# A sorted-attention and token-mixing kernel: a new order of its units, k' turned by 128-column weights, the last output row in halves

## Chip, cores and metric

The kernel runs on one core of a Trainium2 chip. Its time is the device time of one execution in microseconds (us); lower is better. Each engine (TensorE or PE, VectorE or DVE, ScalarE or ACT, GpSimd or POOL, SyncE or SP) runs its own list of instructions in order and waits on semaphores for the others. TensorE writes to PSUM, which has eight banks; VectorE and ScalarE copy results from there to SBUF.

## What is computed

For 4 batches and 8 heads, keys and values of 8 blocks of 96 positions are mixed by an 8 x 8 matrix that five rounds of row and column normalization have made; each block of queries then attends to its mixed block. The result is the input of a token mixer.

```python
for _ in range(5):                      # P = sort_net, 4 x 8 x 8 x 8
    P = exp(P - P.max(-1))
    P = P / P.sum(-1);  P = P / P.sum(-2)
k_sorted = einsum('bhij,bhjcd->bhicd', P, k_b)      # q, k, v: 4 x 8 x 768 x 64
v_sorted = einsum('bhij,bhjcd->bhicd', P, v_b)
attn = softmax(q_b @ k_sorted^T / 8)                # in blocks of 96
x = attn @ v_sorted                                 # 4 x 768 x 512
W_tok = (x @ w_q) @ (x @ w_k)^T / 8                 # 768 x 768 for each batch
out = relu(W_tok @ x) @ w_out                       # 4 x 768 x 512, float32
```

## The kernel before

The program is a list of units, `ORDER` (lines 20 to 54), which the loop at lines 661 to 671 walks once. A unit is `kind batch number : engine : bank`; a capital letter other than R, D, I is work of TensorE, with the PSUM bank that it writes (K, Y, V, S, P and H take two banks from there on). A small letter is mostly the copy that takes the result of the same capital out of that bank; A is ScalarE, D VectorE, G GpSimd, S SyncE. So `K20:6` turns the keys of batch 2, heads 0 and 1, into banks 6 and 7, and `k20:A:6` lets ScalarE copy them out. Each engine gets its units in the order of the list, and waits are put in by the framework for every tile, bank and buffer that two units share. The order thus decides everything: which unit of TensorE stands behind which, which engine copies, which bank is used again how soon, and what is queued behind what on a DMA queue.

The kinds, in the order in which a batch goes through them:

- `l`: a load by GpSimd's queue of half the heads of q, k or v of a batch (`lk2a`: k, batch 2, first half); I: the loads of q of batch 0 by SP. `lp` and `lo` load the mixer's weights.
- A, a, c, B, u, n: the normalization and the matrices M that sort (VectorE and ScalarE alternate: a is exp, c the sums and quotients). Z are idle products with zeros, beside that chain.
- p, z (copies), Q, q: queries, two heads at a time, turned by TensorE.
- K, k: sorted and turned keys. V, v: sorted values, which R (six transfers by SP) puts into VT; for batch 0 Y, y, F, f do the same on TensorE.
- S, e: scores of five head pairs and blocks at a time, and exp to E (line 363).
- P, r, x: E times the values, the reciprocal of the row sums and the quotient to X (lines 387, 392). There are five such groups, the fifth of 8 instead of 14 products.
- T, t (batches 0 and 1) or D (batches 2 and 3, a transposing transfer by SP, line 398): X turned to XT. D20 needs the groups 0 to 2, D21 the groups 2 to 4.
- J, j: the mixer's q' and k' (qkT, 64 rows each) for half of the positions, from all four parts of XT. d copies k' to other partitions (qD).
- W, w (`u_W`, line 423): k' turned back, block by block, by a product of a 96-column piece of qkT, taken as weights, with part of an identity.
- G, g, H, h: k'^T x, and its product with q', then the relu, to mixT.
- O, o, s: the output rows, six of 128 positions for a batch: four products of 512 columns, a copy to a buffer `ot` (four of them, used in turn, each for two rows), and a store. Batches 0 to 2 store two rows at a time (512 KB), batch 3 each row by itself (256 KB). `osplit` (line 464) reads a number over 9 as a half row: `O325` is batch 3, row 5, second half.

Batches overlap: the attention of batch b+1 stands between the mixer units of batch b. A check on the row sums (`guard`, line 495) and a path for its failure, which doesn't run here, close the program.

## Time and profile before

| | |
|---|---|
| time before, median of 3 runs | 98.08 us (97.96 to 98.28) |
| the profiled execution | 98.33 us |
| its span, first to last instruction | 96.4 us |
| TensorE busy | 86.3 us, 1333 products |
| weight loads (PEld, beside TensorE) | 58.7 us |
| VectorE, ScalarE, GpSimd busy | 72.6, 68.8, 43.1 us |
| mean granted clock of TensorE | 0.991 |
| read from and written to HBM | 20.19 and 6.29 MB |

In the profile's rows, `ps<-wo,mixT 128*128 128x512` is a product that writes PSUM from weights of 128 partitions by 128 columns and 512 columns of data; behind `|` stand the busy time in us and the mean length of one in ns, then the idle time before them with what ended it. Products overlap, so that the distance of their starts, not their length, is what one costs. `SPq` is SP's queue, `POOLq` GpSimd's. A tile's name stands without its buffer number. Line 154 is the helper of all products, lines 158, 160 and 162 are the copies of ScalarE, GpSimd and VectorE.

### The profile page before, as it was taken

The page shows a single profiled execution, that of the slowest core. Times are in us where ns is not written, and L with a number is a line of the kernel's source. Part 1 is how long each engine was busy: PE and PEld are TensorE (multiplying, and loading weights), DVE is VectorE, ACT ScalarE, POOL GpSimd, SP SyncE. Part 2 cuts the span into 40 slices and gives each one's busy share as a digit, 9 for nine tenths or more (in the row PEclk, how much of TensorE's full clock was granted, in tenths as well). Part 3 has the DMA queues.
Part 4 walks back from the last instruction along what each step waited for, and adds up shares of the span by engine and source line. Part 5 has one row for each costly group of instructions (what it writes and reads, how often), then busy time and mean ns, then how long its engine had stood idle before and what let it go on. Part 6 is the DMA issues. An engine that isn't in the chain of part 4 may idle for free.

```text
span 96.4 us, 3206 instructions
## 1 busy us (share of the span) xinstructions
PE 86.3 (90%) x1333; PEld 58.7 (61%) x1342; DVE 72.6 (75%) x141; ACT 68.8 (71%) x96; POOL 43.1 (45%) x70
## 2 busy tenths in 40 slices
PE   4999587999899999999999999899969999999930
PEld 2344177788787687845778687674756545644400
DVE  2767896988999469999877999987796773645520
ACT  5177629998979999796989888999746090466220
POOL 6996309700999993049998006000004021950000
PEclk9999999999999999999999999999999999999996
DMA  0899999999999999999999999379953899785992
GB/s 10 266 353 227 203 203 203 203 203 207 195 275 216 209 203 207 202 204 249 250 225 204 202 204 289 124 208 206 205 206 70 199 118 413 289 352 221 396 366 112
DMA packets 24655, 21.44 MB, mean 222 GB/s; under 512 B 7296, under 2 KB 22720, under 8 KB 24640
## 3 DMA queue, kind: packets, MB, share of 16 engines
q0 software_dynamic: 12720, 10.36, 65.5%
q1 hardware_dynamic: 11200, 9.05, 35.5%
q10 hardware_dynamic: 720, 1.84, 4.8%
q8 instruction: 10, 0.16, 0.7%
q14 instruction: 5, 0.04, 0.1%
HBM read 20.19 MB, written 6.29 MB: 275 GB/s over the span
## 4 chain that ended last, share of the span: by engine, by line
PE 55%; DVE 16%; ACT 12%; DMA 10%; issue 3%; SPq 0%; DVEq 0%; ACTq 0%
PE ps L154 55%; DMA XT<-X 5%; DMA XT<-in_q_dram 5%; DVE X L392 4%; ACT E L363 4%; ACT KT L158 3%; DVE QT L162 2%; ACT Vs L158 2%; DVE VT L162 1%; DVE Vs L162 1%; DVE M L253 1%; DVE XT L162 1%; ACT mixT L460 1%; ACT Qn L158 1%; DVE tmp L193 1%
## 5 line engine op out<-in xcount | busy, mean ns | idle before, releaser
L363 ACT ACTIVATE E<-ps 96x960 bf16<-96x960 f32 (+1 forms) x28 | 24.3, 905 | 2.2 <-PE ps L154 1.6
L154 PE MATMUL ps<-wo,mixT 128*128 128x512 bf16 x88 | 22.8, 380 | 0.4
L392 DVE TENSOR_TENSOR X<-ps,Rall 96x896 bf16<-96x896 f32 (+1 forms) x20 | 20.1, 1006 | 0.7
L160 POOL COPY Qn<-Qn 128x768 bf16<-128x768 bf16 x10 | 8.1, 831 | 16.9 <-DMA Qn<-in_q_dram 16.9
L162 DVE COPY ot<-ps 128x512 f32<-128x512 f32 (+1 forms) x16 | 10.8, 687 | 4.8 <-PE ps L154 4.5
L154 PEld LDWEIGHTS <-mixT 128*128 128x128 bf16 x96 | 8.3, 98 | 9.1 <-issue 0.8
L154 PE MATMUL ps<-VT,E 96*128 96x65 bf16 x256 | 11.2, 193 | 0.3
L154 PEld LDWEIGHTS <-KT 64*128 64x128 bf16 (+1 forms) x288 | 8.4, 97 | 4.5 <-issue 2.2
L154 PEld LDWEIGHTS <-E 96*128 96x128 bf16 x256 | 9.7, 97 | 2.1 <-issue 0.4
L158 ACT CAST KT<-ps 128x768 bf16<-128x768 f32 x13 | 10.2, 808 | 0.9 <-DVE Rall L387 0.4
L154 PE MATMUL ps<-QT,KT 64*128 64x96 bf16 x256 | 9.3, 204 | 1.1 <-ACT KT L158 0.8
L160 POOL COPY qD<-qkT 64x384 bf16<-64x384 bf16 x6 | 3.0, 505 | 15.0 <-ACT qkT L158 12.8
L460 ACT ACTIVATE mixT<-ps 128x1024 bf16<-128x1024 f32 x7 | 7.1, 1027 | 3.5 <-PE ps L154 3.5
L253 POOL TENSOR_TENSOR M<-PTR,m_p 128x512 bf16<-128x512 bf16 x6 | 7.9, 1318 | 3.6 <-ACT PTR L158 3.5
L158 ACT COPY ot<-ps 128x512 f32<-128x512 f32 x9 | 5.3, 587 | 5.1 <-PE ps L154 4.7
L154 PE MATMUL ps<-idb,Qn 128*128 128x128 bf16 x96 | 7.7, 220 | 1.1 <-DVE Pm L190 1.0
L154 PE MATMUL ps<-fil 128*128 128x512 bf16 x25 | 8.2, 482 | 0.1
L154 PE MATMUL ps<-M,Kn 128*64 128x128 bf16 x192 | 7.8, 221 | 0.1
L162 DVE CAST KT<-ps 128x768 bf16<-128x768 f32 x7 | 6.7, 955 | 1.2 <-PE ps L154 1.1
L154 PEld LDWEIGHTS <-Qn 128*128 128x128 bf16 x96 | 5.7, 98 | 3.0 <-ACT Qn L158 2.1
L158 ACT CAST Vs<-ps 128x1024 bf16<-128x1024 f32 x7 | 7.0, 1012 | 0.6 <-PE ps L154 0.5
L387 DVE RECIPROCAL Rall<-ps 96x14 f32<-96x14 f32 (+1 forms) x20 | 4.6, 228 | 3.5 <-PE ps L154 2.2
(84 smaller groups left out, 142.9 us busy)
## 6 DMA issues: line engine op xcount, KB each, us to landing
Vn<-in_v_dram POOLq DMA_DIRECT2D x8, 384.0 KB, 9.6
Kn<-in_k_dram POOLq DMA_DIRECT2D x8, 384.0 KB, 11.4
out_dram<-ot SPq DMA_DIRECT2D x5, 512.0 KB, 4.7
VT<-Vs SPq DMA_DIRECT2D x18, 132.0 KB, 5.0
Qn<-in_q_dram POOLq DMA_DIRECT2D x6, 384.0 KB, 11.4
XT<-in_q_dram SPq DMA_DIRECT2D x2, 768.0 KB, 5.7
out_dram<-ot POOLq DMA_DIRECT2D x2, 512.0 KB, 7.4
out_dram<-ot ACTq DMA_DIRECT2D x2, 512.0 KB, 2.8
```

Of the source, the lines that this page charges most:

```text
L154: nc.tensor.matmul(o, w, x, is_transpose=t, start=start, stop=stop, skip_group_check=True)
L158: nc.scalar.copy(o, i)
L160: nc.gpsimd.tensor_copy(o, i)
L162: nc.vector.tensor_copy(o, i)
L193: nc.vector.reduce_sum(tmp, (Pm if n == 1 else Pv).rearrange("p i j -> p j i"), axis=AX.X)
L253: ENG[e].tensor_tensor(out=M[b % 2][:, h0:h0 + hn], in0=src.unsqueeze(2).to_broadcast([P, hn, SP, NB]), in1=m_p.unsqueeze(1).unsqueeze(3). ...
L363: nc.scalar.activation(E[b % 2][:, n, 0:2 * w * BLK].rearrange("p (t a c) -> p a t c", a=2, c=BLK), PS[0:BLK, bank:bank + 2, 0:w * BLK].re ...
L387: nc.vector.reciprocal(Rall[:, b, n, :, 0:w], avps(bank, w)[:, :, :, D])
L392: nc.vector.tensor_mul(xo.rearrange("p (a t d) -> p a t d", a=2, d=D), avps(bank, w)[:, :, :, 0:D], Rall[:, b, n, :, 0:w].unsqueeze(3).to_ ...
L460: nc.scalar.activation(o, i, ACT.Relu)
```

## The change

There are three edits. `ORDER` is replaced as a whole: the same units, but for the three named below, in another order, with other banks and in 66 places another engine. In it, heads 4 to 7 of batch 0 go first and not last; some y, k and v copies of batches 0 and 1 change between ScalarE and VectorE; s01 and s10 go from GpSimd's queue to SP's, other stores and copies between SP, ScalarE and VectorE; the loads come in another sequence (lq3b is the last one, not lk3b). There are 25 idle products in place of 26 (Z53 for Z54). In `u_W`, three of four pieces of qkT are taken as weights of 128 columns and write 128 rows, of which 96 are used. The last row of batch 3, now row 5 in place of row 3, is computed, copied and stored in two halves of 256 columns (O325, O315 and their o and s).

```diff
--- before.py
+++ after.py
@@ -18,39 +18,39 @@
 VHEAD = set()
 
 ORDER = """
-i00:G i02:D I00:S A00:0 Z04:1 Z15:1 Z25:1 lv0b I01:S lk0a c00:D a01:A i03:G c01:D lv0a a02:A:0 lk0b
-c02:D z11:A lv1b lv1a a03:A Q01:0 Z33:1 c03:D lk1a lq1b lk1b z10:A a04:A c04:D z12:A Q00:2 Z43:1
-q01:D:0 a05:A z13:A c05:D q00:A:2 Z54:1 Q03:0 Z62:1 q03:D:0 B00:2 Q02:3 n01:D:2 n00:D:2 n03:D:2
-u00:A:2 K01:4 K00:0 q02:D:3 n11:G n10:G k01:A:4 Y03:6 k00:D:0 y03:A:6 S02:4 n02:D:2 e02:A:4 Y00:0
-K02:2 Y02:6 y00:A:0 k02:D:2 Y01:4 y02:A:6 S00:0 y01:D:4 lp K03:2 e00:A:0 S01:6 k03:D:2 F00:4 lq1a
-e01:A:6 F01:5 f00:D:4 S06:2 S05:0 e06:A:2 f01:D:5 P00:6 e05:A:0 S03:2 r00:D:6 x00:D:6 V12:4 e03:A:2
-P01:0 r01:D:0 x01:D:0 v12:A:4 S04:6 F03:2 F02:3 e04:A:6 R15:S V11:4 f02:D:3 V10:0 v11:A:4 f03:D:2
-P02:6 p12:G v10:A:0 r02:D:6 x02:D:6 R12:S p13:G P04:2 R14:S K11:4 n20:G T00:0 r04:D:2 x04:D:2
-k11:A:4 R13:S Q12:1 P03:6 R11:S t00:A:0 q12:D:1 lk2a K13:2 r03:D:6 x03:D:6 R10:S Q13:1 k13:A:2 lv2b
-K12:4 U00:0 k12:A:4 lv2a K10:2 z01:D:0 T03:6 q13:D:1 k10:A:2 T02:7 t03:D:6 U01:4 p11:G T01:5 t02:D:7
-z02:A:4 S16:2 S14:0 t01:D:5 lo e16:A:2 S15:6 Q11:4 e15:A:6 p10:G J01:5 q11:D:4 J00:2 e14:A:0 n21:G
-S13:6 j00:D:2 j01:A:5 Q10:0 e13:A:6 W01:1 lq2a W00:1 P14:2 P13:4 w00:A:1 d01:G r14:D:2 x14:D:2
-q10:A:0 K20:6 lq2b G00:1 r13:D:4 x13:D:4 k20:A:6 lq3a S11:2 G01:1 e11:A:2 d00:G K21:6 g00:D:1 S10:4
-lk2b k21:D:6 H01:0 e10:A:4 h01:D:0 V20:2 V21:4 v20:A:2 V22:6 v21:D:4 P10:0 v22:A:6 R21:S T13:2
-r10:D:0 x10:D:0 R20:S H02:4 S12:6 O02:3 R25:S e12:A:6 h02:D:4 R23:S H00:0 o02:A:3 P12:6 R22:S
-h00:A:0 O03:3 p21:G r12:D:6 x12:D:6 R24:S t13:A:2 P11:4 lk3a O04:0 r11:D:4 x11:D:4 p20:G O00:2
-o04:A:0 lv3a p23:A T10:0 o00:D:2 lv3b Q21:1 p22:A Q20:4 q21:D:1 T11:2 n31:G q20:A:4 T12:5 t11:D:2
-O05:1 t12:A:5 o03:D:3 lq3b t10:D:0 S22:6 S20:4 e22:A:6 S21:2 lk3b o05:D:1 J11:0 p30:G e21:A:2 Q23:1
-j11:D:0 J10:6 p31:G q23:D:1 e20:A:4 Q22:7 j10:D:6 W11:1 n30:G Q30:0 q22:A:7 K22:4 q30:D:0 K23:2
-k22:A:4 Q31:0 s01:G k23:D:2 W10:1 P21:6 d10:G w10:A:1 d11:D S23:4 q31:D:0 S24:2 e23:A:4 O01:1
-r21:D:6 x21:D:6 e24:A:2 S25:4 G10:0 o01:D:1 e25:A:4 K31:6 K30:2 k31:D:6 G11:0 k30:A:2 P22:4 g10:D:0
-S26:2 r22:D:4 x22:D:4 V30:0 e26:A:2 P23:6 v30:A:0 H10:2 r23:D:6 x23:D:6 V31:4 h10:A:2 R30:S p33:G
-S31:0 R31:S v31:D:4 e31:A:0 p32:G V32:6 H12:2 v32:A:6 S32:0 h12:D:2 R33:S Q33:4 Q32:5 e32:A:0 R32:S
-K32:6 q33:D:4 R34:S P24:2 k32:A:6 K33:0 r24:D:2 x24:D:2 R35:S k33:A:0 P20:6 q32:D:5 D21:S H11:2
-S35:0 r20:D:6 x20:D:6 h11:A:2 O14:5 e35:A:0 S33:2 o14:D:5 D20:S S36:6 O13:4 e33:A:2 P31:0 s00:S
-e36:A:6 S34:2 r31:D:0 x31:D:0 P34:6 e34:A:2 O10:5 r34:D:6 x34:D:6 P32:2 o10:A:5 S30:0 r32:D:2
-x32:D:2 P33:6 e30:A:0 J20:5 J21:0 r33:D:6 x33:D:6 j20:A:5 P30:2 d20:G j21:A:0 W20:5 r30:D:2 x30:D:2
-d21:G W21:5 D31:S O12:6 w20:A:5 G21:5 o13:D:4 D30:S G20:5 o12:D:6 O11:4 g20:D:5 s11:S H20:6 s02:S
-H22:2 h20:A:6 H21:0 h22:D:2 O15:5 o11:A:4 O21:6 o15:D:5 h21:A:0 s10:G O20:7 J30:0 J31:1 j30:D:0
-O25:5 d30:G j31:D:1 d31:S W30:4 o20:D:7 W31:4 O22:1 w30:A:4 w31:A:4 o25:D:5 o21:A:6 G31:0 s12:A
-G30:0 s20:A O23:6 o22:A:1 g30:A:0 H30:0 o23:D:6 H31:4 h30:A:0 H32:2 h31:D:4 O24:7 s21:S h32:A:2
-O31:6 o24:A:7 O32:2 o31:D:6 s22:S O34:3 s31:A o32:D:2 O35:6 s32:A o34:A:3 O30:7 o35:D:6 s34:S O33:3
-s35:A o30:D:7 s30:S o33:A:3 s33:S
+i00:G i02:D I01:S A00:0 lk0b I00:S Z04:1 lv0b c00:D a01:A lv0a c01:D Z15:2 i03:G a02:A:0 lk0a c02:D
+z13:A lv1a Z25:0 lv1b a03:A c03:D lk1b z12:A Q03:2 a04:A Z33:3 c04:D Q02:0 z10:A Z43:3 q03:D:2 a05:A
+z11:A Z53:1 c05:D Q00:2 Z62:1 q00:A:2 q02:D:0 B00:1 Q01:2 n02:D:1 n03:D:1 q01:A:2 K02:4 n01:D:1
+K03:6 k02:A:4 n00:D:1 Y02:2 u00:D:1 k03:A:6 Y01:4 y02:D:2 lq1b n11:G Y00:0 y01:A:4 S05:6 y00:D:0
+K01:2 e05:A:6 Y03:4 n10:G F02:0 y03:D:4 k01:A:2 K00:6 f02:D:0 S04:4 k00:A:6 F00:2 lp e04:A:4 S03:0
+f00:D:2 F01:6 e03:A:0 F03:7 lq1a f01:D:6 S01:4 S02:2 f03:D:7 lk1a e01:A:4 V10:0 P03:6 v10:D:0
+e02:A:2 K13:4 S00:2 r03:D:6 x03:D:6 k13:A:4 R11:S P01:0 e00:A:2 V11:4 r01:D:0 x01:D:0 K12:6 v11:A:4
+p12:G P02:2 k12:A:6 r02:D:2 x02:D:2 n21:G R13:S S06:4 P00:0 e06:A:4 R12:S V12:6 r00:D:0 x00:D:0
+P04:4 p13:G v12:A:6 U00:2 Q12:3 lk2a q12:A:3 R15:S T02:6 r04:D:4 x04:D:4 Q13:7 p11:G R14:S T00:0
+z01:A:2 q13:D:7 T01:1 lv2a t02:A:6 R10:S T03:2 t00:D:0 S15:4 t01:D:1 lv2b S16:6 U01:3 e16:A:6 K11:0
+z02:D:3 p10:G e15:A:4 K10:6 k11:D:0 Q11:3 lo t03:A:2 S14:4 q11:D:3 Q10:0 lq2a e14:A:4 J01:1 q10:D:0
+k10:D:6 S13:2 S12:4 e13:A:2 J00:0 j01:D:1 P14:6 e12:A:4 j00:D:0 S11:2 r14:D:6 x14:D:6 W01:1 d00:G
+W00:1 P12:4 w00:A:1 n20:G S10:6 e11:A:2 r12:D:4 x12:D:4 G01:1 G00:1 e10:A:6 lk2b K21:2 g00:D:1 P13:4
+n31:G d01:D k21:A:2 H00:6 r13:D:4 x13:D:4 H02:0 h00:A:6 V20:2 n30:G h02:D:0 v20:A:2 H01:6 T13:4 lq3a
+T12:5 h01:A:6 R21:S V21:2 t12:D:5 V22:0 R20:S v21:A:2 P11:6 O05:5 r11:D:6 x11:D:6 v22:A:0 R23:S
+O01:2 p21:G R22:S o05:D:5 P10:6 R25:S p20:G o01:A:2 O02:0 r10:D:6 x10:D:6 R24:S t13:A:4 lq2b Q20:1
+lv3b K22:4 q20:D:1 K20:6 k22:A:4 lv3a T11:2 k20:D:6 Q21:1 t11:A:2 O03:4 lk3a q21:D:1 o02:A:0 lk3b
+T10:5 S21:0 t10:D:5 S20:2 e21:A:0 S22:6 o03:D:4 J11:5 p30:G e20:A:2 K23:0 p31:G J10:4 k23:D:0
+j11:A:5 e22:A:6 Q30:2 d11:G Q31:5 q30:D:2 P20:0 p23:A p22:G q31:D:5 O04:6 r20:D:0 x20:D:0 j10:A:4
+lq3b Q23:7 W11:4 Q22:5 q23:A:7 o04:D:6 W10:4 P21:0 w10:A:4 q22:D:5 S26:2 S25:6 e26:A:2 r21:D:0
+x21:D:0 G11:4 e25:A:6 G10:4 S23:2 g10:D:4 P24:6 e23:A:2 d10:D S24:0 r24:D:6 x24:D:6 V30:4 e24:A:0
+V32:2 v30:D:4 V31:6 v32:A:2 K31:0 v31:D:6 R31:S P22:4 k31:A:0 K30:2 R30:S r22:D:4 x22:D:4 H10:0
+k30:A:2 R34:S O00:6 h10:A:0 R35:S S31:2 o00:D:6 S32:4 R32:S e31:A:2 P23:0 p33:G R33:S K32:6 r23:D:0
+x23:D:0 e32:A:4 D20:S O10:2 p32:G k32:A:6 Q33:3 o10:D:2 H12:0 s02:S q33:A:3 S30:4 H11:6 D21:S Q32:2
+e30:A:4 h11:D:6 O11:3 h12:A:0 q32:D:2 K33:4 o11:D:3 P31:6 k33:A:4 S33:0 r31:D:6 x31:D:6 s10:S
+e33:A:0 S34:2 s01:S P30:4 s00:S e34:A:2 r30:D:4 x30:D:4 O13:0 P32:6 S36:4 S35:2 r32:D:6 x32:D:6
+e36:A:4 J20:1 e35:A:2 J21:4 D30:S j20:A:1 P33:6 j21:D:4 d20:G P34:2 r33:D:6 x33:D:6 W20:1 W21:1
+O12:4 w20:A:1 o13:A:0 G20:5 r34:D:2 x34:D:2 o12:A:4 G21:5 d21:D O14:0 D31:S g20:A:5 H20:4 o14:D:0
+H22:2 h20:A:4 H21:6 s11:S O15:1 h21:D:6 O20:0 h22:D:2 O22:6 o15:D:1 O21:7 o22:A:6 s12:S J31:6 J30:1
+j31:A:6 W31:2 j30:D:1 O23:6 w31:A:2 d31:A d30:D W30:2 o23:D:6 G31:1 w30:A:2 G30:1 o20:D:0 s21:A
+O24:6 o21:A:7 g30:D:1 s20:S H30:0 o24:D:6 H31:2 h30:A:0 H32:4 h31:D:2 O25:7 h32:A:4 O31:6 o25:D:7
+O33:4 s22:A o31:A:6 O32:5 s31:A o33:A:4 O34:6 o32:D:5 s33:A O30:7 s32:S o34:D:6 O325:5 s34:S o30:A:7
+O315:4 o325:A:5 s30:S o315:A:4 s325:S s315:S
 """
 
 
@@ -422,7 +422,8 @@
 
     def u_W(b, n, bank):
         for i in range(4 * n, 4 * n + 4):
-            mm(PS[0:BLK, bank, i * DH:(i + 1) * DH], qkT[b % 2][:, i * BLK:(i + 1) * BLK], idb[:, DH:P])
+            w = BLK if i % 4 == 3 else P
+            mm(PS[0:w, bank, i * DH:(i + 1) * DH], qkT[b % 2][:, i * BLK:i * BLK + w], idb[:, DH:P])
 
     def u_w(b, n, e, bank):
         i0, i1 = (4 * n, 4 * n + 4) if b == B - 1 else (0, NB)
```

## Prediction

> **What bounds the kernel now.** I read the page's busy times first, then the busy time by stretches, then the chain that ended last, then the timelines of TensorE and of SP's queue around its long pieces.
>
> ```profile
> span 96.4 us, 3206 instructions
> ...
> PE 86.3 (90%) x1333; PEld 58.7 (61%) x1342; DVE 72.6 (75%) x141; ACT 68.8 (71%) x96; POOL 43.1 (45%) x70
> ```
>
> TensorE is busy for 86.3 of 96.4 us, so a new order can only take away its gaps, or add some. The stretches say where the gaps are; behind each pair of bounds stand the length and then the busy time of PE, PEld, DVE, ACT and POOL.
>
> ```profile
> 12.14:34.00 21.86, 20.24 (x459) 17.33 (x460) 18.59 (x32) 19.03 (x26) 14.07 (x17) 1.00 1.28 213
> 55.00:71.57 16.57, 15.30 (x302) 11.35 (x303) 14.71 (x24) 14.66 (x18) 1.59 (x2) 1.00 1.04 203
> 80.10:92.50 12.40, 12.29 (x83) 6.08 (x83) 7.01 (x10) 5.00 (x9) 3.74 (x8) 1.00 0.83 334
> ```
>
> From the first product after the normalization (12.14 us) to 34 us TensorE is idle for 1.62 us, from 55 to 71.57 for 1.27 us, and in the last 12.4 us for 0.11 us. The granted clock is 1.00 throughout (the column behind POOL). The second stretch has two pieces with a name:
>
> ```profile
> 60.54 0.61 PE L154 MATMUL ps<-Vn,M 128*128 128x128 bf16 x8 [0.35 <-DVE X L392]
> ...
> 63.96 0.59 PE L154 MATMUL ps<-VT,E 96*128 96x65 bf16 x14
> ...
> 66.47 1.04 PE L154 MATMUL ps<-wo,mixT 128*128 128x512 bf16 x4
> 67.34 0.60 PE L154 MATMUL ps<-VT,E 96*128 96x65 bf16 x14
> ...
> 70.30 0.59 PE L154 MATMUL ps<-VT,E 96*128 96x65 bf16 x14
> 71.57 1.47 PE L154 MATMUL ps<-XT,wqk 128*128 128x384 bf16 x8 [0.68 <-DMA XT<-X]
> ```
>
> The first row is V32, which waits 0.35 us for x23 to leave bank 6. Then come P20, the output row O13 (67.34 - 66.47 = 0.87 us for its four products), P31, P33, and last J20 with J21. The chain that ended last shows why J20 is late: it goes through the second transposing transfer of batch 2 (D20), which takes 5.19 us of it.
>
> ```profile
> 66.33 5.19 DMA XT<-X
> ```
>
> **Part 1, the order on TensorE: switches.** A row of the trace gives the price of going from one shape of product to another.
>
> ```profile
> 33.05 0.39 PE L154 MATMUL ps<-QT,KT 64*128 64x96 bf16 x10
> 33.37 0.51 PE L154 MATMUL ps<-idb,Qn 128*128 128x128 bf16 x6
> 33.72 0.51 PE L154 MATMUL ps<-idb,qkT 128*96 128x64 bf16 x8
> 34.06 0.84 PE L154 MATMUL ps<-VT,E 96*128 96x65 bf16 x22
> 34.84 0.36 PE L154 MATMUL ps<-M,Kn 128*64 128x128 bf16 x6
> ```
>
> ```profile
> 48.37 0.81 PE L154 MATMUL ps<-QT,KT 64*128 64x96 bf16 x30
> 49.11 0.50 PE L154 MATMUL ps<-XT,wqk 128*128 128x384 bf16 x2
> ```
>
> Ten score products that stand alone (S13) hold TensorE from 33.05 to 33.37, 0.32 us. Three such units in a row (S22, S20, S21) hold it for 0.74 us. If one unit costs a and leaving the scores costs s, a + s = 0.32 and 3a + s = 0.74, so a = 0.21 and s = 0.11; I take 0.095 for a switch, since a semaphore's share is in it. The kinds fall into three classes: S and H (weights on 64 rows), K, Y, G and the first U (weights of 64 columns), and all others. Counting changes of class along the list gives 69 in the old order and 74 in the new one. Five more at 0.095 are **+0.47 us**; in gaps they cost nothing, so the other end is 0.
>
> **Part 2, k' by 128-column weights (u_W).** 24 of the 32 weight loads grow from 96 to 128 columns.
>
> ```profile
> L154 PEld LDWEIGHTS <-E 96*128 96x128 bf16 x256 | 9.7, 97 | 2.1 <-issue 0.4 <-ACT E L363 0.2
> ```
>
> ```profile
> L154 PE MATMUL ps<-idb,qkT 128*96 128x64 bf16 x32 | 2.3, 208 | 0.0
> ...
> L154 PEld LDWEIGHTS <-qkT 128*96 128x96 bf16 x32 | 2.0, 124 | 0.3
> ```
>
> A load of 128 columns takes 97 ns here, one of 96 columns 124 ns. The spacing agrees: in the timeline above, 8 W products with one product's length of 0.21 us (208 ns) taken off 0.51 us come every 0.043 us, and 22 P products behind 128-column weights (0.84 us) every 0.030 us. So each longer load spares up to 0.013 us, 24 of them at most 0.31 us. Only a product whose load follows another W product shows it, so I take **-0.15 us**, with 0 and -0.31 as ends. The Trainium skill says the opposite in "TensorE: Matmul & The Clock Gate", section "LDWEIGHTS (loading the stationary operand)": a load's time is its columns divided by 1.2, so that 128 columns cost 107 ns against 80 ns. By that rule the edit would cost an estimated 24 x 0.027 = 0.64 us, and the total below would be 0.79 us higher; the two rows contradict it.
>
> **Part 3, the wait of J20.** P33's 14 products at 0.030 us end at 70.30 + 0.43 = 70.73 us, and J20 starts at 71.57: 0.84 us lost, until D20 has landed. In the old order the work from P20 (63.96) to J20 is 70.73 - 63.96 = 6.8 us long, while P20's way through x20 and D20 takes 71.57 - 63.96 = 7.6 us. In the new order the last such way begins at P23, and until J20 TensorE has three output rows, as before, five score units and three P, but also K32, K33, Q33 and Q32, and one more H, for one P less of eight products. The two K are 24 products at (0.36 - 0.21)/5 = 0.03, the two Q 12 at (0.51 - 0.21)/5 = 0.06: 1.4 us more work, and 0.4 us of switches that Part 1 counts. That makes 8.2 us or more against 7.6 us. I take **-0.8 us**; the other end is 0, if the transfers come later (second rival).
>
> **Part 4, the wait of V32.** V32 goes to bank 2, which e23 on ScalarE frees, and stands ahead of P22 and P23, so x23 no longer holds it up: **-0.35 us**, other end 0. Next in line is V31, now behind x24, the short one. I give nothing for the smaller gaps of that stretch.
>
> **Part 5, the opening.** The idle products drop from 26 to 25; they lie beside the normalization's chain on VectorE and ScalarE, which has the same steps in the same order with one QT copy at the same place in it, so 12.14 us stays. Without that cover each would be worth one 512-column product. Behind it work is moved between engines. Of the large copies VectorE takes over y00, y02, y03, k10, k11 and v10, and gives away y01, k00, k02 and k03.
>
> ```profile
> L162 DVE CAST KT<-ps 128x768 bf16<-128x768 f32 x7 | 6.7, 955 | 1.2 <-PE ps L154 1.1
> ...
> L162 DVE CAST Vs<-ps 128x1024 bf16<-128x1024 f32 x2 | 2.4, 1213 | 0.0
> ```
>
> One more KT copy and a Vs copy are +0.96 + 1.21 = +2.2 us; five small ones against four make it 2.2 to 2.7. VectorE then has 20.8 to 21.3 of the 21.86 us. ScalarE loses about as much and its chain of E comes sooner. I take **0**: the lower end is -0.6, a third of the gap of 1.62, the upper one is the first rival.
>
> **Part 6, the end.** Behind TensorE's last product only ScalarE's copy of the last row and SP's store are left. The row is now copied and stored in halves, both copies on ScalarE and both stores on SP.
>
> ```profile
> L158 ACT COPY ot<-ps 128x512 f32<-128x512 f32 x9 | 5.3, 587 | 5.1 <-PE ps L154 4.7 <-ACT ot L158 0.5
> ...
> L158 ACT CAST wk<-ps 96x256 bf16<-96x256 f32 x2 | 0.6, 370 | 3.2 <-PE ps L154 3.2
> ```
>
> The last copy shrinks from 587 to some 370 ns, -0.22 us. TensorE's eight half products are the same columns as four whole ones. A half store moves half as much, but SP has one store more to issue: between -0.2 and +0.15, I take 0. Together **-0.2 us**. Other transfers and copies moved to other engines between 71.57 and 92.5 us (d31 to ScalarE, stores between SP and ScalarE) lie beside a TensorE that is 99% busy from 80.10 us on; I cost them at nothing, and at their own length if that cover is gone.
>
> **The sum:** +0.47 - 0.15 - 0.8 - 0.35 + 0 - 0.2 = -1.03 us. The profiled execution took 98.33 us (96.4 us of span and 1.9 us around it), so its counterpart would be 97.3; it lies 0.25 us above the median of 98.08, which goes to 97.05, and I forecast **97.0 us**. Its own range is 96.3 to 97.7 us: one of the larger parts, 0.6 to 0.8 us, at its other end.
>
> **Rivals.** *VectorE becomes the bound in the opening (slower).* It now waits 21.86 - 18.59 = 3.27 us in that stretch. With 2.2 to 2.7 us more work only 0.6 to 1.1 us of waiting fit in. Against it: a longer queue waits less. If the waits stay, the stretch grows by 2.4 us: 99.4 us. It decides from about 0.9 us of waits on.
>
> *SP's queue makes J20 and J31 late (slower).* Old and new stores and transposes lie in this queue:
>
> ```profile
> 64.58 3.33 SPq L398 DMA_TRANSPOSE XT<-X  x2
> 67.96 0.74 SPq L485 DMA_DIRECT2D out_dram<-ot  x1
> 72.85 3.44 SPq L398 DMA_TRANSPOSE XT<-X  x2
> 76.39 2.15 SPq L485 DMA_DIRECT2D out_dram<-ot  x2
> ```
>
> ```profile
> XT<-X SPq DMA_TRANSPOSE x1, 4.0
> XT<-X SPq DMA_TRANSPOSE x1, 5.2
> out_dram<-ot SPq DMA_DIRECT2D x1, 512.0 KB, 4.7
> ```
>
> D21, issued at 64.58, lands at 68.6; D20, issued at 66.33, at 71.5; s00, issued at 67.96, at 72.7. So in line each transpose takes 2.9 us and a store 1.2 us. The new order has D20 s02 D21 s10 s01 s00 D30 D31 in one line; s01 and s10, until now POOL's, wait in front of D30 and D31. From an issue at about 62.5 us (it waits for x22 and for the last VT transfer, where D21 now waits for x24 until 64.58; an estimate) that is 4.0 + 3 x 2.9 + 4 x 1.2 = 17.5, so D31 lands at 80.0 us, about when J31 is due by my forecast (J30 starts at 80.10 now, and an output row of 0.87 us has moved ahead of it). The gain is gone when it lands after 81; at 0.5 us more for each of the four, 82.0 us, the time is 98.9 us.
>
> *Nothing changes:* the waits of Parts 3 and 4 come back elsewhere, on copies that now stand behind others: 97.05 + 0.8 + 0.35 = 98.2 us. For it speaks that DVE and ACT are busy for 89% and 88% of the stretch where both lie. *The opening gains too:* 96.2 us, or less. *Loads cost by their columns:* 128/96 of 124 ns is 165 ns, 41 ns more for each of 24, +1.0 us in place of -0.15: 98.2 us. This is the rule of the Trainium skill named in Part 2; the 97 ns row speaks against it.
>
> **How the numbers follow.** Forecast 0.52, a gain in the opening as well 0.08, loads by their columns 0.02, no change 0.12, VectorE 0.14, SP's queue 0.12. A change under 0.3% (0.3 us) can't be told from none here. Faster is 0.60, the same 0.14, slower 0.26. The range from 96.0 to 99.0 us leaves out about 0.15, above all the first rival.
>
> **What would show it.** Right: J20 and V32 without a wait, J31 at about 80 us, W's loads at 97 ns, 74 changes of class, and P14 at 34 us as before. Wrong: P14 much later than 34 us with VectorE full from 12 to 34 us (first rival), J20 or J31 released by the transfer of X (second), or new waits of TensorE for ScalarE and VectorE between 45 and 70 us (third).

## The result: slower by 6%

| | before | after |
|---|---|---|
| median, same chip | 98.28 us (97.96 to 99.04, 5 runs) | 104.24 us (103.80 to 106.41, 5 runs) |
| ratio, 95% interval | | 1.0605 (1.0551 to 1.0659) |
| profiled execution, its span | 98.33 us, 96.4 us | 103.8 us, 101.6 us |
| mean granted clock of TensorE | 0.991 | 0.975 |

The forecast was 97.0 us. The page of the changed kernel has the span, the busy times and the row of the granted clock:

```profile
span 101.6 us, 3221 instructions
...
PE 87.3 (86%) x1335; PEld 59.5 (59%) x1345; DVE 73.8 (73%) x142; ACT 69.9 (69%) x99; POOL 41.3 (41%) x66
...
PEclk9999999999999999999999999999995899999996
```

TensorE is busy for 1.0 us more, and the span is 5.2 us longer, so most of the loss is idle time. This execution is the fastest of the five runs of the changed kernel. One new thing stands in the clock's row: a 5, three quarters of the way through. The view by stretches says where the time is:

```profile
12.07:35.96 23.89, 20.83 (x463) 17.17 (x462) 20.40 (x34) 20.21 (x26) 13.94 (x18) 1.00 1.23 204
35.96:55.00 19.04, 17.58 (x315) 13.28 (x318) 15.11 (x23) 14.92 (x20) 13.52 (x17) 1.00 1.24 207
55.00:73.20 18.20, 17.65 (x344) 13.06 (x344) 16.47 (x28) 15.69 (x21) 2.15 (x3) 1.00 0.99 173
73.20:79.80 6.60, 4.66 (x45) 3.02 (x42) 3.55 (x6) 2.71 (x5) 0.95 (x2) 0.74 0.99 330
...
86.08:97.80 11.72, 11.66 (x84) 5.97 (x83) 6.26 (x10) 6.25 (x11) 0.00 (x0) 1.00 0.62 251
```

Behind the bounds and the length stand, as in the prediction, the busy times of PE, PEld, DVE, ACT and POOL, and then the granted clock. Up to P14 (35.96 us) TensorE is idle for 3.06 us; before it was 1.62 us up to the same unit. From there to 55 us it is idle for 1.46 us. Then comes the stretch that the change was to shorten, and it is good: 0.55 us in 18.2, where there were 1.27 us in 16.57. From J20 (73.20 us) on everything is lost at once: 1.94 us idle in 6.6 us, and the granted clock is 0.74 on average. The end is as full as before. The long waits of TensorE have one row each in its timeline:

```profile
22.35 0.53 PE L154 MATMUL ps<-M,Kn 128*64 128x128 bf16 x12 [0.98 <-DMA Kn<-in_k_dram]
...
35.96 0.42 PE L154 MATMUL ps<-VT,E 96*128 96x65 bf16 x8 [1.47 <-DMA VT<-Vs]
...
40.65 0.27 PE L154 MATMUL ps<-qD,Ab 64*128 64x256 bf16 x1 [0.67 <-DVE qD L162]
...
59.70 1.51 PE L154 MATMUL ps<-Vn,M 128*128 128x128 bf16 x24
...
73.20 0.50 PE L154 MATMUL ps<-XT,wqk 128*128 128x384 bf16 x2
75.42 1.57 PE L154 MATMUL ps<-XT,wqk 128*128 128x384 bf16 x6 [1.72 <-DMA XT<-X]
76.78 1.42 PE L154 MATMUL ps<-VT,E 96*128 96x65 bf16 x22
```

These are K13, P14, H02, the three V units of batch 3 (no wait between them now: V32's is gone), and J20 with J21. J20's first two products start at 73.20 without a wait, and the third, which reads the part of XT that D21 fills, stands until 75.42 us. Behind it 22 P products take 1.23 us (from 76.78 to 78.01, where W starts); at the 0.030 us for each of the old profile they would take 0.66 us.

The chain that ended last now runs through those transfers. The second number is the length of a piece:

```profile
7.19 15.11 DMA Kn<-in_k_dram
...
22.35 0.55 PE ps L154 x12
...
22.91 0.80 ACT KT L158
...
26.88 1.02 ACT Vs L158
...
29.32 6.59 DMA VT<-Vs
...
35.96 1.56 PE ps L154 x40
...
39.39 1.22 DVE qD L162
...
69.11 6.26 DMA XT<-X
```

The load of k for heads 4 to 7 of batch 1 releases K13; ScalarE's copies behind it end with the last Vs copy at 27.9 us; the last of the six VT transfers (R10) is issued at 29.32 us and lands 6.6 us later, at 35.91; P14 starts. Before, it was issued at 27.51 us and landed at 32.67, 1.4 us ahead of P14, which started at 34.06. Then d01, a copy of VectorE, takes 1.2 us, and at the end D21 takes 6.3 us. (By the code a d copies q', rows 0 to 63 of qkT, for the H products, and not k', as the list of kinds has it.) SP's queue shows what stood ahead of D21 (start, length of the issue):

```profile
66.81 1.58 SPq L398 DMA_TRANSPOSE XT<-X  x1
68.44 0.57 SPq L486 DMA_DIRECT2D out_dram<-ot  x1
69.11 2.29 SPq L398 DMA_TRANSPOSE XT<-X  x1
71.59 2.47 SPq L486 DMA_DIRECT2D out_dram<-ot  x3
74.33 7.14 SPq L398 DMA_TRANSPOSE XT<-X  x2
```

D20, the store s02, D21, three more stores, D30 and D31: the line that the second rival named. The granted clock around J21 stands third from the end, in stretches of 1 us:

```profile
75.00:76.00 1.00, 0.58 (x4) 0.38 (x4) 0.00 (x0) 0.00 (x1) 0.00 (x0) 0.99 1.10 455
76.00:77.00 1.00, 1.00 (x8) 0.52 (x7) 0.00 (x0) 0.47 (x1) 0.40 (x1) 0.50 0.97 397
...
78.00:79.00 1.00, 0.78 (x13) 0.72 (x12) 0.97 (x2) 0.28 (x1) 0.00 (x0) 0.50 1.06 343
79.00:80.00 1.00, 1.00 (x5) 0.30 (x6) 0.96 (x3) 0.89 (x3) 0.65 (x1) 0.80 1.26 283
```

For 3.4 us TensorE runs at half its clock, so the wait for D21 is paid nearly twice: once as idle time, and then up to 1.7 us as slow products. Two stretches of the kernel before are needed for the sum:

```profile
71.57:80.10 8.53, 8.48 (x78) 4.74 (x80) 5.91 (x9) 3.97 (x6) 1.55 (x3) 1.00 0.82 163
34.00:55.00 21.00, 20.50 (x369) 15.14 (x369) 18.38 (x30) 18.61 (x25) 13.40 (x18) 1.00 1.28 217
```

Up to P14 there is 1.4 us more idle time (3.06 - 1.62), from there to 55 us 1.0 us more (1.46 - 0.50), up to J20 0.7 us less, then 1.9 us more (1.94 - 0.05) and 1.2 us of half clock (4.66 us busy x 0.26): 4.8 of the 5.2 us. The other 0.4 us is not assigned; five more switches less what W gains would be 0.3 us by the prediction's prices (0.47 - 0.15), which no run isolates. The sum is that of this one execution.

### The profile page after: what moved, and what is told of

The parts are those of the page before. It is cut to its first block, busy times and chain, and to the rows that moved or that the text cites. A ratio compares the mean times of both kernels' runs of the same rounds, so it can differ in the third digit from the quotient of the medians.

```text
span 101.6 us, 3221 instructions
## 1 busy us (share of the span) xinstructions
PE 87.3 (86%) x1335; PEld 59.5 (59%) x1345; DVE 73.8 (73%) x142; ACT 69.9 (69%) x99; POOL 41.3 (41%) x66
## 4 chain that ended last, share of the span: by engine, by line
PE 42%; DMA 28%; DVE 10%; ACT 6%; POOL 6%; issue 3%; SPq 1%; DVEq 0%; POOLq 0%
PE ps L154 42%; DMA Kn<-in_k_dram 15%; DMA VT<-Vs 6%; DMA XT<-X 6%; POOL Vn L232 3%; DVE X L392 3%; ACT Vs L158 2%; POOL Kn L232 2%; DVE qD L162 1%; SPq L330 1%; DVE mixT L463 1%; DVE Vs L162 1%; DVE QT L162 1%; ACT mixT L461 1%; DVE Rall L387 1%
## 5 line engine op out<-in xcount | busy, mean ns | idle before, releaser
L154 PE MATMUL ps<-wo,mixT 128*128 128x512 bf16 (+1 forms) x91 | 22.7, 373 | 0.9 <-ACT E L363 0.3
L160 POOL COPY Qn<-Qn 128x768 bf16<-128x768 bf16 x11 | 9.0, 835 | 14.3 <-DMA Qn<-in_q_dram 7.3
L154 PEld LDWEIGHTS <-mixT 128*128 128x128 bf16 x100 | 9.0, 99 | 9.7 <-issue 1.9
L154 PE MATMUL ps<-VT,E 96*128 96x65 bf16 x256 | 11.7, 198 | 1.9 <-DMA VT<-Vs 1.5
L162 DVE COPY ot<-ps 128x512 f32<-128x512 f32 x14 | 9.5, 686 | 4.7 <-PE ps L154 4.5
L158 ACT COPY ot<-ps 128x512 f32<-128x512 f32 (+2 forms) x12 | 6.5, 552 | 6.2 <-PE ps L154 4.9
L154 PE MATMUL ps<-QT,KT 64*128 64x96 bf16 x256 | 8.8, 204 | 0.3 <-ACT Vs L158 0.2
L160 POOL COPY qD<-qkT 64x384 bf16<-64x384 bf16 x3 | 1.5, 502 | 18.2 <-ACT qkT L158 15.5
L154 PE MATMUL ps<-XT,wqk 128*128 128x384 bf16 x32 | 6.8, 343 | 1.7 <-DMA XT<-X 1.7
L154 PEld LDWEIGHTS <-Kn 128*64 128x64 bf16 x192 | 5.9, 109 | 2.8 <-DMA Kn<-in_k_dram 1.1
```

The source lines that it names most:

```text
L154: nc.tensor.matmul(o, w, x, is_transpose=t, start=start, stop=stop, skip_group_check=True)
L158: nc.scalar.copy(o, i)
L160: nc.gpsimd.tensor_copy(o, i)
L162: nc.vector.tensor_copy(o, i)
```

## The experiments

Seventeen kernels in four groups. Ratios are against the kernel before on the same chip (its median there 98.1 to 98.5 us), with a 95% interval.

### One wait at a time in the new order

**The VT transfers.** The last transfers are issued right behind the first of their pair:

```diff
- R11:S ... R13:S ... R12:S ... R15:S ... R14:S ... R10:S
+ R11:S R10:S ... R13:S R12:S ... R15:S R14:S
```

> The changed kernel with one transfer moved: R10 is issued right behind R11 and not as the last of the six transfers to VT of batch 1. Theory 1 (the last VT transfer sets P14): the last transfer is now R14, issued at about 28.5 us in place of 29.3, and P14, at 35.96 us in the changed kernel, comes 0.7 to 1.2 us earlier; the later stages lose their own waits as before, so the time falls by 0.5 to 1.2 us from 104.2. Rival (the stages behind absorb it, because D21 sets the time): P14 comes earlier, the time falls by less than 0.3 us. Rival (the load of k, K13 at 22.35 us, sets it): P14 stays within 0.3 us of 35.96.

Measured: 104.48 us, ratio 1.0569 (1.0501 to 1.0637). P14 started at 34.49 us and had almost nothing left of its wait, so the transfers did set it. But the time stayed (104.24 us with the change): H02 now waited for d01, as the timeline of this kernel shows.

```profile
37.78 2.57 POOL L253 TENSOR_TENSOR M<-PTR,m_p 128x512 bf16<-128x512 bf16 x2
...
37.92 2.55 DVE L162 COPY qD<-qkT 64x384 bf16<-64x384 bf16 x1
...
40.52 0.37 PE L154 MATMUL ps<-qD,Ab 64*128 64x256 bf16 x1 [2.01 <-DVE qD L162]
```

A copy that takes 0.25 us elsewhere took 2.55 us, over the whole of GpSimd's two products; then the clock fell to half for two such stretches (7 us).

**d01 earlier**, ahead of those products:

```diff
- j00:D:0 S11:2 ... n31:G d01:D
+ j00:D:0 d01:D S11:2 ... n31:G
```

> The changed kernel with VectorE's copy d01 moved ahead, from behind g00 to right behind j00, where VectorE is idle for 1.3 us. Theory 3 (the copy takes 1.21 us in place of 0.255 because GpSimd makes M beside it, and holds up H00 and x13): H02 starts 0.7 to 1.0 us earlier relative to P14, and O05 0.8 to 1.2 us; the time falls by 0.3 to 1.0 us. Rival (H00 has another wait just behind, on k21 or x13): H02 moves by less than 0.3 us, the time by less than 0.2.

Measured: 102.58 us, ratio 1.0322 (1.0255 to 1.0389). H02's wait was gone, d01 took 0.25 us. That is more than the theory's 0.3 to 1.0 us, by the ratios 2.8% of the time before. In its profile, which is of its slowest run (103.86 us), P14 waited 2.30 us for VT, and the half clock came behind that.

**Idle products before J20:**

```diff
- e36:A:4 J20:1
+ e36:A:4 Z08:1 J20:1
```

> The changed kernel with eight idle products of 512 columns (1.7 us) in front of J20, where TensorE otherwise waits for D21 from about 73.5 to 75.4 us. Theory 2 (the granted clock falls to 0.5 because TensorE stands idle there): the clock stays at 1.0 from 72 to 80 us, J21 ends at the same time and the units from J21 to G20 lose 1.0 to 1.4 us; the time falls by about 1.2 us. Rival (the clock falls for another reason, or the loss is the wait itself): the clock still shows 0.5 in that stretch, the time stays within 0.3 us of 104.2 or grows by up to 0.5.

Measured: 105.82 us, ratio 1.0726 (1.0678 to 1.0774). The clock stayed full behind J21, but the gain of 1.2 us did not come: the eight idle products cost 1.7 us themselves, and in the profile P14 waited 3.4 us. As a price of the half clock this run told little.

**D21 ahead of s02:**

```diff
- D20:S ... s02:S ... D21:S ... s10:S
+ D20:S ... D21:S s02:S ... s10:S
```

> The changed kernel with the store s02 moved behind D21 on SP's queue. Theory 4 (D21 is late because SP's line holds a store of 512 KB in front of it): D21, issued at 69.11 and landed at 75.38 us, is issued at about 68.5 and lands 1.2 to 1.8 us earlier; J20's wait goes, and with it the fall of the clock, so the time falls by 2 to 3 us. Rival (D21 can't start before x23, which ends at 66.7 us, and takes 5 to 6 us whatever stands in front of it): it lands at most 0.6 us earlier, the time falls by under 0.8 us.

Measured: 105.77 us, with runs from 102.57 to 108.09, so no gain that can be told. The spread goes with the clock: the run of 102.57 us had a mean of 0.996, the three others 0.931 to 0.966. In the profile, which is of the slowest, J21 waited only 0.2 us, as expected, and D21's way was 5.1 us in place of 6.3; but the stores behind D21 came later, and O14 waited 1.97 us for bank 0, which o13 could only leave when s00 had emptied its buffer.

What follows from the four: each wait is real. In the first and the last of them another late unit waited in its place, H02 and O14. And P14's wait is not one number: up to P14 three of these kernels (d01 earlier, the idle products, D21 first) have the changed kernel's order, as has GpSimd's products later, further down. Their profiles show 2.30, 3.44, 1.92 and 2.71 us where the changed kernel's shows 1.47, each time behind a last VT transfer of 6.9 to 8.0 us, and the clock fell behind each of the four.

### Parts of the change, and its faults, on the kernel before

**128-column weights alone** (the new `u_W` of the change, the old `ORDER`):

> The kernel before with one part of the change alone: k' turned by 128-column weights. Forecast from the 97 and 124 ns rows: the weight loads fall from 124 to 97 ns, and the time falls by 0.15 us (0 to 0.31 us). Rival (a load costs by its columns): the loads rise to 107 ns or more against the others, and the time rises by 0.6 to 1.0 us.

Measured: 97.99 us against 98.25, ratio 0.9983 (0.9957 to 1.0009). Groups by form, and a W unit in the timeline (its eight products now hold TensorE from 33.71 to the next unit at 34.06):

```profile
L154 PEld LDWEIGHTS <-qkT 128*128 128x128 bf16 x24 | 1.3, 98 | 0.3
...
L154 PEld LDWEIGHTS <-qkT 128*96 128x96 bf16 x8 | 1.0, 124 | 0.0
```

```profile
33.71 0.43 PE L154 MATMUL ps<-idb,qkT 128*128 128x64 bf16 x8
```

The longer load is the shorter one, 98 against 124 ns, and the unit takes 0.43 us in place of 0.51.

**The end in halves alone:**

```diff
- O33:3 s35:A o30:D:7 s30:S o33:A:3 s33:S
+ O323:3 s35:A o30:D:7 O313:4 s30:S o323:A:3 o313:A:4 s323:S s313:S
```

> The kernel before with one part of the change alone: the last output row of batch 3 as two halves of 256 columns, each with its own copy on ScalarE and its own store on SP. Forecast: the last copy takes 370 ns instead of 587 ns, the last store is issued 0.2 us sooner after TensorE's end, and the time falls by 0.2 us. Rival (the second store's issue behind the first takes it back): no change within 0.1 us, or up to 0.15 us slower.

Measured: 98.48 us, ratio 1.0027 (0.9998 to 1.0056): no gain. SP issues four stores in a row:

```profile
91.16 2.87 SPq L488 DMA_DIRECT2D out_dram<-ot  x4
```

The row holds pauses too; one issue takes 0.33 to 0.48 us. The last half's store starts 0.58 us behind the first half's, at 93.62 us, 0.5 us after its copy's end (93.14 us); before, the whole row's was issued 0.02 us after it.

**A store between the transposes of the old order:**

```diff
- D21:S ... D20:S ... s00:S
+ D21:S ... s00:S D20:S
```

> The kernel before, with one store (s00, output rows 0 and 1 of batch 0) issued on SP's queue between the transposes D21 and D20 instead of behind both. Theory (a store in this queue holds back the transpose behind it, as s02 did to D21 in the new order): D20 lands 1.2 us or more later than 71.5 us, J20's wait grows from 0.8 us to 2.0 us or more; without a fall of TensorE's clock the time is 99.5 us, with one of a whole 3.4-us stretch at half clock (1.7 us of lost work) about 101 us. Rival (store and transpose run side by side, and D21 was late in the new order for another reason): J20's wait stays at 0.8 to 1.0 us and the time at 98.3 us.

Measured: 100.67 us, ratio 1.0188 (1.0115 to 1.0260): one store, moved ahead of D20 in SP's queue, costs 1.9 us by the ratio (1.1 to 2.6), 2.4 us by the medians. TensorE's timeline, then its clock behind the wait:

```profile
72.48 2.05 PE L154 MATMUL ps<-XT,wqk 128*128 128x384 bf16 x8 [1.59 <-DMA XT<-X]
```

```profile
73.00:74.00 1.00, 1.00 (x5) 0.48 (x4) 0.00 (x0) 0.48 (x1) 0.00 (x0) 0.61 0.00 0
74.00:75.00 1.00, 1.00 (x14) 0.83 (x13) 0.00 (x0) 0.43 (x1) 0.50 (x1) 0.50 1.04 242
...
76.00:77.00 1.00, 0.78 (x3) 0.29 (x2) 1.00 (x2) 0.56 (x1) 0.00 (x0) 0.68 0.00 0
```

J20 starts at 72.48 us in place of 71.57: 0.9 us by the wait. The rest goes with the half clock. D20's way in the chain of this kernel was 5.8 us, where it was 5.19 us before:

```profile
66.67 5.76 DMA XT<-X
```

**The same with that wait filled:**

```diff
- s00:S D20:S ... P33:6 e30:A:0 J20:5
+ s00:S D20:S ... P33:6 e30:A:0 Z07:5 J20:5
```

> The kernel before with s00 between D21 and D20 (100.67 us; J20 waited 1.73 us, and then TensorE's granted clock was 0.5 for 3.6 us), and seven idle products of 512 columns (7 x 0.216 = 1.5 us) ahead of J20, in the time in which it waits. Theory (the wait itself costs 0.9 us more than in the kernel before, the rest is the half clock that TensorE's idleness brings): J20 starts at the same time, the clock stays at 1.0, and the time is 99.2 us. Rival (the clock falls for another reason, or what follows J20 is late anyway): 100.5 us or more.

Measured: 99.74 us, ratio 1.0127 (1.0067 to 1.0186): 1.2 us over the kernel before by the ratio in place of 1.9, between the theory's time and the rival's. J20 started later still in its profile, because D20 landed later (73.00 us in place of 72.43); the view ends at 74 us and so shows six of the eight products:

```profile
73.04 1.14 PE L154 MATMUL ps<-XT,wqk 128*128 128x384 bf16 x6 [0.64 <-DMA XT<-X]
```

```profile
74.00:75.00 1.00, 1.00 (x22) 0.86 (x19) 0.03 (x1) 0.88 (x2) 0.45 (x1) 1.00 1.07 247
```

The idle products kept the clock at 1.00, and not in this profile alone: the mean clock of the four runs is 0.997 to 1.000 with them and 0.973 to 0.991 without. So the clock falls because TensorE is idle. That the fall has a price of its own is seen in the profiles (a span of 97.8 us with them and 98.8 without, although J20 starts 0.56 us later); the times alone don't show it, since the two intervals overlap.

### Two causes by themselves

**Both early, VT and d01** (the first two diffs together):

> The new order with two steps put elsewhere: the VT transfers that the batch-1 product units need last are issued in the order R11 R10 R13 R12 R15 R14, and d01, VectorE's copy of qkT into qD, stands right behind j00 instead of behind the M products on GpSimd. Theory (each long wait of TensorE costs itself and, where it is over about 1.7 us, up to 1.7 us of half clock behind it): taken alone, the first step moved P14 by 1.5 us but left the time at 104.5 us, because H02 then waited 2.3 us for d01; the second alone gave 102.6 us while P14 waited 2.5 us. Together P14's wait falls below 0.5 us, H02's below 0.2 us, TensorE keeps its full clock between 34 and 50 us, and the time is 100.0 to 101.5 us. Rival (the waits are only passed on to the next late unit, so the order as a whole is too tight): 102.5 to 104 us, with P20 or J21 waiting longer by what was gained.

Measured: 101.65 us, ratio 1.0296 (1.0223 to 1.0368), just over the theory's range; the profile has a full clock from 12 us on. P14 still waited 1.0 us, with the last VT transfer on its way for 6.9 us.

**Loads later**, to see why these transfers are long: with the last kernel's edits,

```diff
- lk2a ... p11:G ... lv2a ... lv2b ... p10:G ... lo
+ p11:G ... p10:G lk2a lv2a lv2b lo
```

> The kernel with VT transfers and d01 early (101.65 us, last VT transfer of batch 1 issued at 28.8 us and landed 6.9 us later), with the loads of batch 2's k and v and of w_out issued behind GpSimd's last copy p10, 1.5 to 2.5 us later. Theory (a VT transfer shares the DMA engines with the loads that are under way, so it is long where three or four loads were issued around it): the last VT transfers take 5.0 to 5.5 us, as in the kernel before, P14 waits under 0.4 us, and the time is 100.3 to 101.0 us, unless V20 then waits for its own load. Rival (the transfers' length does not hang on these loads): 6 to 7 us again, P14 waits 1.1 us, the time is 101.6 us.

Measured: 100.51 us, ratio 1.0248 (1.0206 to 1.0291). The issues of the last two VT transfers (R15 and R14), first without and then with this edit; the last number is the median time to landing:

```profile
VT<-Vs SPq DMA_DIRECT2D x2, 132.0 KB, 6.2
```

```profile
VT<-Vs SPq DMA_DIRECT2D x2, 132.0 KB, 3.2
```

The transfers are long where loads are issued around them: 3.2 us without, less than the theory's 5.0, and P14 waited no more. The change had put the transfers, late by a K13 that waits for its load, among three loads. A few tenths decide: in the run with all four steps, further down, GpSimd came to these loads sooner; R15, issued 0.8 us ahead of the first of them, took 3.3 us, and R14, 0.2 us ahead of it, took 6.0. What the step gives in time is not shown: the interval overlaps with that of the run without it.

**GpSimd's products later, d01 in its place.** In the changed kernel itself:

```diff
- n31:G d01:D ... n30:G ... p21:G
+ d01:D ... p21:G n31:G n30:G
```

> The new order with GpSimd's two M products for batch 3 (n31 and n30, 1.3 us each) moved behind p21, that is, away from VectorE's copy d01, which stays where the change put it. In the changed kernel d01 took 1.21 us instead of 0.25 us and ended 0.1 us behind n30, and H02 waited 0.86 us for it. Theory (VectorE's copy from SBUF to SBUF doesn't run while GpSimd's product does): d01 takes 0.25 us, H02 waits under 0.1 us, and the time falls by 0.9 to 2 us, to 102.3 to 103.4 us. Rival (d01 is late because of its place in VectorE's queue): it takes over 1 us again or H02 still waits 0.5 us or more, and the time stays at 104.2 us.

Measured: 105.27 us (103.66 to 106.86). P14 waited 2.7 us in the profile, so that d01 came only at 42.4 us; it took 0.25 us, but this run could not tell what it was for. With the VT transfers early:

> The kernel with VT transfers early alone (104.48 us; VectorE's copy d01 took 2.55 us from 37.92 us on, beside GpSimd's products n31 and n30 from 37.78 to 40.35 us), with these two products moved behind p21; d01 keeps its place in VectorE's queue. Theory (the copy doesn't run while GpSimd's products do): d01 starts at about the same time and takes 0.25 us, H02 waits under 0.2 us instead of 2.3 us, the half clock behind it is gone unless P14 waits long, and the time is 101 to 102.2 us. Rival (d01 is slow at that place for another reason): 2 us and more again, 104 us or more.

Measured: 101.39 us, ratio 1.0301 (1.0250 to 1.0352), 3.1 us under the same kernel without the edit (ratio 1.0569). VectorE's timeline:

```profile
38.65 0.25 DVE L162 COPY qD<-qkT 64x384 bf16<-64x384 bf16 x1
```

The place in the queue is the same, the copy ten times shorter. It does not run while GpSimd's products do. VectorE's work out of PSUM does: in the changed kernel its quotient x13 took the usual 1.09 us beside the first of the two products. The Trainium skill states the like ("SBUF — State Buffer", section "Who interferes with whom"): a copy of VectorE can run in a mode of two ports, in which it needs a port pair that it shares with GpSimd, and whoever issues first holds the pair for the whole instruction. The trace agrees as to the waiting (that the copy ran in this mode no run shows), and adds that both of GpSimd's products went first: 2.55 us is the length of two (2.57), and 1.21 us in the changed kernel the rest of the second one.

### All together

**The stores out of the transposes' line** (with VT and d01 early):

```diff
+ ... o03:D:4 s01:G ... o04:D:6 s02:G ... D20:S ... D21:S s00:S ... s10:S ...
- ... D20:S ... s02:S ... D21:S ... s10:S ... s01:S ... s00:S ...
```

> The kernel with VT transfers and d01 early (101.65 us; its profile has a full clock from 12 us to the end, and TensorE waits there for J21 1.5 us, P14 1.1 us, K13 0.9 us, O14 0.7 us, P20 0.6 us), and the stores of batch 0 taken out of the line ahead of D21 and behind it: s01 and s02 on GpSimd's queue as soon as their rows are copied, s00 on SP's directly behind D21. Theory (the line of stores and transposes is what makes J21 and O14 late): J21 waits under 0.3 us, O14 no more, D30 and D31 land 2 us sooner, and the time is 99.4 us (98.9 to 100.2). Rival (D21 is late for its own reasons, or other waits take the place): 101 to 102 us.

Measured: 99.44 us (98.50 to 101.52), ratio 1.0120 (1.0070 to 1.0171), as the theory had it. J20 and J21 have one row, without a gap:

```profile
71.71 1.48 PE L154 MATMUL ps<-XT,wqk 128*128 128x384 bf16 x8
```

**P14 and K13 later, on top of that:**

```diff
- K13:4 S00:2 ... P01:0 ... P14:6 ... S11:2 ... W01:1 ... W00:1 P12:4 ... S10:6 ... G01:1 G00:1
+ S00:2 ... P01:0 K13:4 ... S11:2 ... W01:1 ... W00:1 P14:6 P12:4 ... G01:1 G00:1 S10:6
```

> The same with two waits of the opening filled with work: P14 moved behind S11, W01 and W00 (and S10 behind G01 and G00), K13 moved behind S00 and P01 with K12 next to it. Theory (these units stand ahead of the transfers they need, VT's and the load of k for heads 4 to 7 of batch 1): P14 and K13 wait 0.3 us or less each, and the time is 1.2 to 1.7 us under that of the run with the stores early, near 98.0 us (97.3 to 98.8), the time of the kernel before. Rival (what is moved behind them only waits in their place, for its copies): within 0.4 us of the run with the stores early.

This run says nothing about the time: the edit moved P14 but left r14 and x14 ahead of it in the list, so these read old sums, the program took the guard's other path, and the time was 75,558 us. In the first 97 us of its profile the waits had not gone either (S00 0.7, S06 0.7, P14 0.9 us).

**The four steps together** (VT, d01, loads, stores; s01 behind d11):

> The new order with all the steps that helped alone: VT transfers of batch 1 in the order R11 R10 R13 R12 R15 R14, d01 behind j00, loads of batch 2's k and v and of w_out behind p10, and the stores of batch 0 out of the line of D21 (s00 behind D21, s01 and s02 on GpSimd's queue, s01 behind d11 so that GpSimd's copies p30 and p31 don't wait for it; where they did, in the profile of the run with the stores early, Q30 and Q31 waited 1.2 us). Theory (the change lost its time in P14, H02, J21, O14 and the half clock behind such waits, and in nothing else): TensorE's waits behind 12 us come down to those of the kernel before or less, the clock stays full, and the time is 97.9 us (97.2 to 98.7), against 104.2 us with the change and 98.2 us before. Rival (the new class changes and the fuller VectorE cost as well): 99 us or more.

Measured: 98.41 us against 98.09, ratio 1.0051 (1.0020 to 1.0081). That is inside the theory's range: of the 6%, half a per cent is left. This run does not separate the shares of the four. The page and TensorE's timeline at J20:

```profile
span 96.1 us, 3230 instructions
...
PE 86.3 (90%) x1345; PEld 58.4 (61%) x1345; DVE 72.5 (75%) x142; ACT 69.8 (73%) x99; POOL 42.5 (44%) x68
```

```profile
71.42 1.47 PE L154 MATMUL ps<-XT,wqk 128*128 128x384 bf16 x8
```

**The last row whole again in that kernel:**

```diff
- O325:5 s34:S o30:A:7 O315:4 o325:A:5 s30:S o315:A:4 s325:S s315:S
+ O35:5 s34:S o30:A:7 s30:S o35:A:5 s35:S
```

> The run with all four steps, with the last output row whole again instead of in halves. Forecast of the halves: the whole row is 0.2 us slower. Rival (the second half's store waits for SP to issue the first, so the halves give nothing; alone in the kernel before they came out at 1.0027 of its time, 0.9998 to 1.0056): within 0.1 us, or the whole row up to 0.3 us faster.

Measured: 98.70 us, ratio 1.0056 (1.0024 to 1.0087), the same as with halves within the noise.

**Four units exchanged with a neighbour in it** (S10 with G01, T13 with H01, P31 with S33, O13 with P32):

> The run with all four steps (98.41 us; its profile still has waits of TensorE for P31 0.6 us, O13 0.5 us, H01 0.4 us and S10 0.3 us), with four units changed in place with a neighbour: S10 behind G01, T13 ahead of H01, P31 behind S33, O13 behind P32. Theory (each unit stands just ahead of the copy or transfer that frees it, and the neighbour is ready): these waits fall by 1.0 us together or more and the time is 97.4 us (97.0 to 98.0), under that of the kernel before. Rival (the copies behind the exchanged units come later by as much): 98.2 to 98.6 us.

Measured: 98.64 us, ratio 1.0046 (1.0019 to 1.0073): nothing. Other units waited in their place (T13 0.4, Q33 0.4, P32 0.6 us), so the rival holds, though it wasn't followed to each copy. No version here beats the kernel before by more than the weights alone may do.

## Why the prediction was wrong, point by point

**The step that failed is Part 5, the opening, taken as 0, and with it the view of Part 3's transfers.** Part 5 costed the large copies of VectorE and ScalarE and nothing of the transfers that these copies release. What lay on the path was the chain load of k (heads 4 to 7), K13, ScalarE's copies, the last VT transfer, P14. The step was -0.6 to 0 (or the first rival); the stretch up to P14 grew by 2.0 us, 1.47 of them P14's wait. R10 was issued 1.8 us later (29.32 against 27.51) and was 1.4 us longer on its way (6.59 against 5.16), together 3.2 us, of which the old order had 1.4 us to spare. The old profile had both to show: the landing of the loads in their order, and how little lay between the last VT transfer and P14.

**First rival (VectorE the bound in the opening): wrong too, though its figure came near by luck** (2.0 us more in the stretch where it said 2.4). VectorE has 20.40 of 23.89 us there, so it waits 3.5 us, about as much as before, and a transfer released P14. In the run with all four steps VectorE has the same work there, 19.79 us, and the stretch is 21.98 us long, as before (21.86).

**Part 5 again, d01.** Of the 66 moves between engines the prediction costed the large copies of the opening, by their durations, and those from 71.57 us on, at nothing. d01 is among neither: 0.25 us long wherever nothing stood beside it, it took 1.21 us, 2.55 us in another run, because of what GpSimd does beside it. No row of the old trace showed a VectorE copy of this kind beside a GpSimd product, and the prediction did not bound it.

**Part 3, J20's wait: the path through P was right, the transfers were not.** The -0.8 us was a way of 7.6 us against 8.2 us or more of work. The work came as forecast: from P23 (64.61 us) to J20 (73.20) it is 8.6 us. The way, from P23 to D21's landing at 75.38, is 10.8 us. J20 itself starts without a wait; its third product waits 1.7 us, and the half clock follows. The second rival had the mechanism and the place (a line of stores and transposes in SP's queue), but it looked for the loss at D30 and D31, whose line it saw ending at 80.0 us. D31 landed at 84.8 us and cost nothing, since TensorE came to J31 only at 86.08 us. What came late was D21, third in that line: the rival's own prices (4.0 + 1.2 + 2.9 us from an issue at 62.5) put it at 70.6 us, but D20 was issued at 66.81 and D21 landed at 75.38. So the prices held (8.6 us in place of 8.1), and the early issue, an estimate, was 4.3 us off. D20 did not wait for x22, which ended at 64.10, but stood behind the VT transfers of batch 3 in SP's queue, whose last issue ended at 66.71. With all four steps it was issued at 63.16: most of the 4.3 us came from the opening.

**No step had the clock.** The forecast priced a wait at its length. Here one of 1.72 us brought 3.4 us of half clock. Behind 20 us, in all profiles of this case, waits of up to 1.47 us were not followed by it (P14's in the changed kernel is one), and of those from 1.59 us on all but one were followed by it. The exception is in the run with D21 ahead of s02:

```profile
58.36 0.59 PE L154 MATMUL ps<-VT,E 96*128 96x65 bf16 x14 [1.71 <-DMA VT<-Vs]
```

The profiles say why. In each, the granted clock changes only on a grid of 3.41 us, and what goes with a fall is how long TensorE was busy in the cell of this grid just ahead: 1.70 us in the changed kernel (72.56 to 75.98 us), 1.76 and 1.96 in the two others with a J20 or H02 wait, 0.20 to 1.98 us ahead of all ten falls within the programs. Cells at full clock with 2.00 us and more kept it, and the wait of 1.71 us lies across a bound (57.38 us), with 2.68 and 2.44 us busy in its two cells. Two of the ten falls, near 13 us, have only shorter waits ahead of them. No run varied the phase of this grid on purpose, and one cell in the last products of a program (1.75 us) was not followed by a fall.

**What held.** Part 4: V32's wait is gone (the row of 24 products at 59.70 us). Part 2: the loads take 98 ns, the sign is right, and 0.2 us (ratio 0.9983) is near the 0.15 forecast, though the interval reaches past 1; the rule of the Trainium skill ("TensorE: Matmul & The Clock Gate", section "LDWEIGHTS (loading the stationary operand)") would by the prediction's estimate have made it 0.64 us slower, which the interval excludes. Part 1: not measured by itself. The best new order is 0.3 us slower than the old one by the medians, 0.5 by the ratio; 0.47 us for switches less what W spares would fit, but waits of other units could make it as well. Part 6: wrong, no gain from halves, neither alone nor in the new order; the copy shrank (372 to 379 ns) as said, and in the profile the second store's issue took it back.

**Settled and open.** Four edits of the new order, none of which touches its arithmetic, bring 104.2 us to 98.4 us: VT transfers behind loads, d01 beside GpSimd, D21 and O14 behind the line of stores, and the half clock behind the first three are the loss. Open are the share of each, what the last 0.3 us is, and why some falls of the clock last one cell of the grid and others two.

## What to carry to other kernels

- A wait of TensorE that a profile of before doesn't have can cost nearly twice its length; look in the clock's row behind every wait of over 1.5 us, and fill it with idle products where the work can't come sooner.
- When an order changes, cost first the transfers: for each unit that needs one, the latest issue, what is queued ahead of it, and which loads are under way beside it. The copies' busy time says little.
- A copy moved from GpSimd to VectorE isn't priced by its row alone; look at what GpSimd runs at that moment.
